# Loading x in four row blocks (12, 8, 8, 4) in a cached grouped-query attention kernel

## The chip, the cores and the metric

The kernel runs on one core of one Trainium2 chip. The metric is the device time of one execution in microseconds (us). The kernel before was run five times; in one more view, a profiled execution shows every engine's instructions and every DMA packet.

## The reference, cut to what matters

Decoding attention over a cache of keys and values, for 8 sequences with 4 new tokens each, 32 query heads, 8 key/value heads, a cache of 2048 positions, head size 128, all in bf16:

```python
B, Sq, D = 8, 4, 512
Hq, Hkv, Sk, Dh = 32, 8, 2048, 128
q = (x @ wq).reshape(B, Sq, Hq, Dh).transpose(0, 2, 1, 3)
k = jnp.repeat(k_cache, rep, axis=1)          # rep = 4
v = jnp.repeat(v_cache, rep, axis=1)
scores = jnp.einsum("bhqd,bhkd->bhqk", q, k) * (Dh ** -0.5)
p = softmax(scores, axis=-1)
o = jnp.einsum("bhqk,bhkd->bhqd", p, v)
out = o.transpose(0, 2, 1, 3).reshape(B, Sq, Hq * Dh) @ wo
```

x has 32 rows of 512 numbers (32 KB); wq and wo have 4 MB each, the two caches 32 MB each.

## The kernel before, in words

**Units.** The work is cut into 32 units, one for each pair of key/value heads and each sequence: for each of four pairs p, all eight sequences b. A unit reads one k tile and one v tile of 1 MB (`load_k`, L111, and `load_v`, L121), each 128 partitions with 8 KB. There are 7 buffers for k tiles and 6 for v tiles.

**Stages of a unit.** TensorE transposes the k tile (L195, two bf16 numbers taken as one fp32), VectorE or ScalarE copies the result to SBUF (L202, L200), TensorE multiplies it by the queries (`scores`, L256), ScalarE takes the exponential (L266), TensorE sums the probabilities (`norms`, L294) and multiplies by v (`values`, L280), VectorE scales (L311). The values of a unit run six half-units behind its scores. The output projection (`project`, L376) is added up in one PSUM tile over the four pairs; its last part waits for the rows of `wo` that are loaded last (`load_wo`, L141).

**The queries.** x (T = 32 rows, one per token) is transposed by four small TensorE operations (L210) into `xT_sb` (copy at L213), then 128 matmuls with wq (L219) give the queries, which ScalarE scales (L226). Four matmuls (L234) and eight copies (L243) lay them out as the block-diagonal `q_bd` that `scores` needs. All of this stands in TensorE's program after the transposes of the first k tile.

**The loads.** All loads are issued by the SP engine in one list. The order is: k of unit 0, wq (4 MB, L144), x (L145), and then what `load_ready` takes from the list `loads`: for the units from 1 on, first one of eight `wo_e` pieces (L131), then the k tile, then, from the fourth on, a v tile. A `wo_e` piece is 5 rows of 12 KB of wo, put on five partitions; it belongs to the rows of wo that the first pair of heads needs. The first `wo_e` piece waits for the memset of `wo_e` on GpSimd (L171). Near the end of the list stand `wo_n` (L134), `wo_m` (L135) and the eight pieces of `wo_sb` (L141). The two halves of the output are stored by ACT (L431) and SP (L432).

**What makes SP wait.** The framework gives the loads eight semaphores in turn, so that each load first waits until the load eight places before it has landed in full. A load into a buffer that is used again also waits for the engine that reads the buffer. The kernel is written with a manual schedule, so each engine's instructions stand in the order in which the code gives them.

The lines that the change touches:

```python
    load_k(0)
    nc.sync.dma_start(wq_sb[:, :, :], wq.rearrange("(p r) n -> p r n", r=R))
    nc.sync.dma_start(x_sb[:, :], x.flatten_outer_dims())
```

Of the kernel before, what the change touches and what calls it, by code (L numbers as in the profile page):

```python
# [14 lines left out]
def kernel(  # L15
# [9 lines left out]
    nc = tc.nc  # L25
# [51 lines left out]
    x_sb = const.tile([T, D], BF16, name="x_sb")  # L77
# [64 lines left out]

    load_k(0)
    nc.sync.dma_start(wq_sb[:, :, :], wq.rearrange("(p r) n -> p r n", r=R))  # L144
    nc.sync.dma_start(x_sb[:, :], x.flatten_outer_dims())  # L145
    loads = []
    for u in range(NU + KA):
        if 1 <= u <= 8:
# [314 lines left out]
```

The softmax here doesn't subtract the row's maximum and nothing guards it: scores larger than these inputs give would overflow.

## Time and profile before

| What | Value |
|---|---|
| Median of five runs | 189.83 us |
| The five runs | 191.86, 189.22, 189.08, 189.83, 192.39 us |
| Profiled execution, its own time | 189.37 us |
| Its span in the trace | 187.6 us |
| TensorE clock granted, mean | 0.979 |
| Bytes read from HBM | 75.53 MB, 403 GB/s over the span |
| Landing of wq / of x, last increment | 15.50 us / 15.69 us |
| First transpose of x on TensorE | 15.74 us |
| First `scores` matmul | 23.27 us |

The span is from the first instruction to the last in the trace; 1.8 us of the execution's own time lie around it. DVE is VectorE, ACT is ScalarE, PE is TensorE, PEld its weight loads, POOL is GpSimd, SP is SyncE; "SPq" is SP's issue of a DMA. A letter L and a number name a line of the kernel. In the row of the 40 slices a digit is the busy share of a slice in tenths. A load's landing is told by increments of its semaphore, one from each DMA engine that takes part in it, and the trace keeps the time of each; it keeps start, length and size of each DMA packet as well, but not the engine's number.

### The profile page before, as it was taken

Reading aid. Unit: us, or ns where it says so; the run is one execution under the profiler, and the core shown is the slowest. Engines: PE = TensorE matmul, PEld = TensorE weight load, DVE = VectorE, ACT = ScalarE, POOL = GpSimd, SP = SyncE. Lnnn points to the kernel's source line nnn. Section 1 sums busy time; section 2 is a strip of 40 time slices with the busy share of each in tenths; the row PEclk is TensorE's granted clock in tenths of the full one; section 3 lists DMA queues with packets and bytes.
Section 4 is the critical chain, followed back from the end, with each engine's and each line's share of the span. In section 5 each row is a group of like instructions: output and inputs, shape, how many; then the busy total and the mean of one; then the engine's idle time right before and its main releaser. Section 6 shows DMA issues by size and latency. Waiting matters only on the chain.

```text
span 187.6 us, 6431 instructions
## 1 busy us (share of the span) xinstructions
PE 154.5 (82%) x2869; PEld 139.1 (74%) x2899; DVE 112.4 (60%) x218; ACT 86.3 (46%) x170; POOL 6.3 (3%) x9
## 2 busy tenths in 40 slices
PE   0535597799999988999999999968888889998672
PEld 0515397699999877889998888857788888886450
DVE  0580544577777666844777666656666667776320
ACT  2003546656556655444565554445554444454000
POOL 8400000000000000000000000000000000000000
PEclk9999979999999999996999999999999999999998
DMA  5999999999999999999999999999999999999970
GB/s 210 461 447 379 424 424 425 427 417 432 425 418 421 426 423 423 430 419 433 421 419 426 428 423 423 421 425 426 421 428 423 426 425 423 423 428 415 406 294 15
DMA packets 10955, 75.97 MB, mean 405 GB/s; under 512 B 1288, under 2 KB 1416, under 8 KB 2568
## 3 DMA queue, kind: packets, MB, share of 16 engines
q1 hardware_dynamic: 10880, 75.55, 96.1%
q8 instruction: 22, 0.36, 0.7%
q14 instruction: 5, 0.04, 0.1%
q10 hardware_dynamic: 48, 0.02, 0.0%
HBM read 75.53 MB, written 0.03 MB: 403 GB/s over the span
## 4 chain that ended last, share of the span: by engine, by line
DMA 97%; SPq 1%; issue 0%; PE 0%; ACT 0%
DMA k_sb<-in_k_cache_dram 69%; DMA v_sb<-in_v_cache_dram 9%; DMA wq_sb<-in_wq_dram 8%; DMA wo_e<-in_wo_dram 7%; DMA wo_sb<-in_wo_dram 4%; SPq L131 0%; PE out_ps L376 0%; SPq L111 0%; ACT out_sb L430 0%; SPq L121 0%
## 5 line engine op out<-in xcount | busy, mean ns | idle before, releaser
L195 PE MATMUL kp<-ident,k_sb 128*128 128x128 f32 x512 | 83.7, 290 | 16.8 <-POOL ident masks.py:199 7.0
L202 DVE COPY kt<-kp 128x1024 bf16<-128x1024 bf16 x96 | 65.2, 684 | 25.3 <-PE kp L195 23.8
L266 ACT ACTIVATE probs<-s_ps 64x256 bf16<-64x256 f32 x128 | 48.4, 378 | 67.1 <-PE s_ps L256 66.3
L195 PEld LDWEIGHTS kp<-ident,k_sb 128*128 128x128 f32 x512 | 56.5, 145 | 19.6 <-DMA k_sb<-in_k_cache_dram 8.2
L256 PE MATMUL s_ps<-q_bd,kt 128*128 128x64 bf16 x1024 | 43.1, 195 | 3.1 <-ACT kt L200 1.9
L256 PEld LDWEIGHTS <-kt 128*128 128x128 bf16 x1024 | 40.6, 100 | 5.5 <-ACT kt L200 2.2
L280 PEld LDWEIGHTS <-v_sb 128*128 128x128 bf16 x1024 | 34.5, 96 | 9.6 <-DMA v_sb<-in_v_cache_dram 2.1
L200 ACT COPY kt<-kp 128x1024 bf16<-128x1024 bf16 x32 | 32.4, 1012 | 12.6 <-PE kp L195 11.8
L280 PE MATMUL o_ps<-probs,v_sb 128*128 128x32 bf16 x1024 | 35.1, 177 | 1.2 <-DMA v_sb<-in_v_cache_dram 1.1
L302 DVE TENSOR_REDUCE l_sb<-l_ps 128x32 f32<-128x512 f32 x32 | 22.1, 692 | 22.0 <-PE l_ps L294 21.7
L294 PE MATMUL l_ps<-probs,ones 128*128 128x512 bf16 x34 | 12.6, 379 | 1.5
L306 DVE RECIPROCAL r_sb<-l_sb 128x32 f32<-128x32 f32 x32 | 11.3, 353 | 1.1
L311 DVE TENSOR_TENSOR oT<-o_ps,r_sb 128x32 bf16<-128x32 f32 x32 | 5.8, 182 | 1.9 <-PE o_ps L280 1.7
L294 PEld LDWEIGHTS <-ones 128*128 128x128 bf16 x64 | 6.1, 98 | 0.5
L430 ACT CAST out_sb<-out_ps 64x256 bf16<-64x256 f32 x1 | 0.4, 366 | 13.1 <-PE out_ps L376 13.1
L171 POOL MEMSET wo_e<- 64x6144 bf16 x1 | 5.2, 5211 | 0.3 <-POOLq L447 0.3
L376 PE MATMUL out_ps<-wo_sb,oP 128*32 128x256 bf16 x48 | 4.1, 274 | 1.4 <-DMA wo_sb<-in_wo_dram 1.4
L243 DVE CAST q_bd<-pse 64x512 bf16<-64x512 f32 x4 | 2.6, 683 | 4.3 <-PE pse L234 4.3
L178 DVE COPY pick<-ident 128x64 bf16<-128x64 bf16 x4 | 0.6, 220 | 6.5 <-POOL ident masks.py:199 6.5
L376 PEld LDWEIGHTS <-oP 128*32 128x32 bf16 x48 | 2.4, 95 | 2.5 <-issue 2.4
L219 PE MATMUL psq<-xT_sb,wq_sb 128*128 128x32 bf16 x128 | 3.5, 186 | 0.3 <-DVE xT_sb L213 0.3
L219 PEld LDWEIGHTS <-wq_sb 128*128 128x128 bf16 x128 | 3.5, 103 | 0.3 <-issue 0.3
(41 smaller groups left out, 31.1 us busy)
## 6 DMA issues: line engine op xcount, KB each, us to landing
k_sb<-in_k_cache_dram SPq DMA_DIRECT2D x32, 1024.0 KB, 19.5
v_sb<-in_v_cache_dram SPq DMA_DIRECT2D x32, 1024.0 KB, 19.4
wq_sb<-in_wq_dram SPq DMA_DIRECT2D x1, 4096.0 KB, 14.3
wo_sb<-in_wo_dram SPq DMA_DIRECT2D x4, 512.0 KB, 14.8
wo_sb<-in_wo_dram SPq DMA_DIRECT2D x4, 256.0 KB, 9.5
wo_m<-in_wo_dram SPq DMA_DIRECT2D x1, 512.0 KB
wo_e<-in_wo_dram SPq DMA_DIRECT2D x8, 60.0 KB
x_sb<-in_x_dram SPq DMA_DIRECT2D x1, 32.0 KB
```

What stands on the lines that cost most here:

```text
L195: nc.tensor.transpose(kp[:, j, :], k4[:, w : w + 128], ident4[:, :])
L200: nc.scalar.copy(out=kt2, in_=kp2)
L202: nc.vector.tensor_copy(out=kt2, in_=kp2)
L219: nc.tensor.matmul(psq[:, h, :], lhsT=wq_sb[:, r, hh * 128 : (hh + 1) * 128], rhs=xT_sb[:, r, :], start=(r == 0), stop=(r == R - 1),)
L256: nc.tensor.matmul(s_ps[:, 2 * j : 2 * j + 2, :], lhsT=k_t[:, j % (HC // 4), :, e], rhs=q_bd[:, p, e, b, :, :], start=(e == 0), stop=(e == 1),
L266: nc.scalar.activation(out=pr[rows, hf * HC : (hf + 1) * HC, cols], in_=s_ps[rows, :, cols], func=EXP)
L280: nc.tensor.matmul(o_ps[u][:, :], lhsT=vs[u][:, cc, :], rhs=pr[:, cc, :], start=(cc == 0), stop=(cc == C - 1),)
L294: nc.tensor.matmul(l_ps[:, :, :], lhsT=ones[:, :], rhs=pr[:, c : c + LC, :], start=(c == 0), stop=(c + LC == C),)
L302: nc.vector.tensor_reduce(out=l_sb[:, :], in_=l_ps[:, :, :].rearrange("d c q -> d q c"), axis=AX, op=ADD)
L306: nc.vector.reciprocal(r_sb[:, :], l_sb[:, :])
L311: nc.vector.tensor_tensor(out=oT[(p + 1) // 2][:, :, (p == 2) * 1, b, :], in0=o_ps[u][:, :].rearrange("d (h s) -> d h s", h=HP), in1=r_sbs ...
L376: nc.tensor.matmul(out_ps[half * T : (half + 1) * T, :], lhsT=o, rhs=w[:, half * DH : (half + 1) * DH], start=(p == 0 and r == 0), stop=(p ...
```

## The change

The load of x is cut into four loads by rows: rows 0 to 11, 12 to 19, 20 to 27 and 28 to 31. They go from the same source rows to the same rows of `x_sb`, in the same place of SP's list, behind wq and ahead of the first `wo_e` piece. Nothing else is changed. In the built programs TensorE, VectorE, ScalarE and GpSimd keep the same instructions in the same order; SP issues three loads more. Lines behind the change move down by two.

```diff
     load_k(0)
     nc.sync.dma_start(wq_sb[:, :, :], wq.rearrange("(p r) n -> p r n", r=R))
-    nc.sync.dma_start(x_sb[:, :], x.flatten_outer_dims())
+
+    for a, n in ((0, 12), (12, 8), (20, 8), (28, 4)):
+        nc.sync.dma_start(x_sb[a : a + n, :], x.flatten_outer_dims()[a : a + n, :])
     loads = []
     for u in range(NU + KA):
         if 1 <= u <= 8:
             loads.append(("e", u - 1))
```

## The prediction

> **What bounds the kernel now.** I read the page from the top (busy shares, the queues, the chain that ended last), then the SP engine's timeline of the first 20 us, where the change sits, and last the trace's records of single DMA packets and semaphore increments. The page first:
>
> ```profile
> span 187.6 us, 6431 instructions
> ...
> PE 154.5 (82%) x2869; PEld 139.1 (74%) x2899; DVE 112.4 (60%) x218; ACT 86.3 (46%) x170; POOL 6.3 (3%) x9
> ...
> DMA  5999999999999999999999999999999999999970
> ...
> q1 hardware_dynamic: 10880, 75.55, 96.1%
> q8 instruction: 22, 0.36, 0.7%
> q14 instruction: 5, 0.04, 0.1%
> ...
> DMA 97%; SPq 1%; issue 0%; PE 0%; ACT 0%
> ```
>
> The DMA row is full from the second slice to the second last, queue q1 alone fills 96.1% of 16 engines' span, and 97% of the chain is DMA. PE is 82% busy and idles for data. So the end is set by bytes through the 16 DMA engines. The windows say the same for the middle (columns: stretch, length, PE, PEld, DVE, ACT, POOL busy, PE clock, DMA share, GB/s):
>
> ```profile
> 40.00:100.00 60.00, 57.30 (x1082) 53.79 (x1095) 42.15 (x85) 33.20 (x67) 0.00 (x0) 0.97 1.01 424
> ```
>
> The chain in order of time ends so (start, length, what):
>
> ```profile
> 176.56 7.53 DMA wo_sb<-in_wo_dram
> 184.09 0.04 issue
> 184.13 0.41 PE out_ps L376 x4
> 184.54 0.02 issue
> 184.56 0.37 ACT out_sb L430
> ```
>
> The last load lands at 184.09; what follows it (four matmuls, one copy, the store) is the same 3.5 us whatever happens earlier.
>
> One level lower: the packet records show every engine back to back. An 8 KB packet takes 309 ns, 12 KB 460 ns, 1 KB 46 ns, the 4 B semaphore packet 9 ns, 16 KB of instructions about 0.95 us. From 14.5 to 18.5 us each chain of packets follows without a gap. The 16 increments of the last load come at 178.8, 178.9, 179.0, 181.3, 181.4, nine between 182.4 and 183.0, 183.88 and 184.09. So the end belongs to one or two engines, and the mean over the 16 is 182.0. Which engines are late can be followed too: each of the eight `wo_e` loads (5 rows of 12 KB) shows five late increments, always behind the same five engines, about 0.45 us each; at 48 us these five land the v load at 47.5 to 47.95, the other eleven at 44.4 to 46.2. The two last engines at the end are, followed load by load, two of these five.
>
> The start, by SP's timeline (start, length of the issue):
>
> ```profile
> 0.73 0.37 SPq L111 DMA_DIRECT2D k_sb<-in_k_cache_dram  x1
> 1.16 0.42 SPq L144 DMA_DIRECT2D wq_sb<-in_wq_dram  x1
> 1.62 0.43 SPq L145 DMA_DIRECT2D x_sb<-in_x_dram  x1
> 5.97 0.84 SPq L131 DMA_DIRECT2D wo_e<-in_wo_dram  x1
> 6.85 0.40 SPq L111 DMA_DIRECT2D k_sb<-in_k_cache_dram  x1
> 7.30 0.72 SPq L131 DMA_DIRECT2D wo_e<-in_wo_dram  x1
> 8.06 0.43 SPq L111 DMA_DIRECT2D k_sb<-in_k_cache_dram  x1
> ...
> 15.52 0.33 SPq L121 DMA_DIRECT2D v_sb<-in_v_cache_dram  x1
> ```
>
> Here SP is idle from 2.05 to 5.97 (the memset of `wo_e` on POOL), and after 9.73 it stands until 15.52:
>
> ```profile
> SPq L121 <- DMA wq_sb<-in_wq_dram: 5.8, 1, 5.8
> ```
>
> In the built program SP's loads take eight semaphores in turn, so load n waits for the full landing of load n-8: the tenth load (v of unit 0) waits for the second (wq, landed at 15.50).
>
> **What the Trainium skill says.** Page "DMA: Bandwidth & Descriptors", section "Why a DMA increments its semaphore by 16 and not by 1": a load issued from SP runs on k engines, the largest k up to 16 that divides the outer sizes, and these are the lowest-numbered k; the sequencer writes the missing 16-k increments at once. The trace agrees on k: `wo_e` with 5 rows shows five late increments and one early, 1.1 to 1.2 us after its issue. That they are the lowest-numbered the trace can't say, only that they are always the same five; I take the page's word. Same page, "Latency and other measured facts": about 600 ns to the first byte from an SP issue; here it is 1.0 us (issue 0.73, first packet 1.73) and 0.85 us for the final store (184.95 to 185.80). Same page, "Rules for kernel authors": under 64 KB one pays mostly overhead. Inside this stream that isn't what one sees: the 32 KB of x cost each engine two 1 KB packets and a semaphore packet, 2 x 46 + 9 = 101 ns, with the next packet directly behind.
>
> **The change, part by part.**
>
> *Bytes on the engines.* Removed: one load of 32 rows on 16 engines, 101 ns of each. Added: loads of 12, 8, 8 and 4 rows, on k = 12, 8, 8 and 4 engines, one row and one semaphore packet (46 + 9 = 55 ns) on each. By the page's rule engines 0-3 take part in all four (220 ns), 4-7 in three (165), 8-11 in one (55), 12-15 in none. The difference is +119, +64, -46 and -101 ns. The five engines that carry `wo_e` are then 0-4, so the two that end last gain +64 to +119 ns. At least one of the two is in 0-3. I take +0.1 us at the end; from both sides 0 and +0.2 (if a packet's gap appears four times instead of once; the increments of x came 0.19 to 0.30 us after those of wq, of which 101 ns was packets).
>
> *Three more issues on SP.* The x issue took 0.43 us, the 5-row `wo_e` issues 0.70 to 0.84; at 0.74 each, four take 3.0 us, from 1.62 to 4.6. `wo_e` waits for POOL until 5.94 anyway. Cost nothing; the cover ends when the four take over 4.3 us.
>
> *Three more places in the eight semaphores.* Numbers of the loads: k0 0, wq 1, x 2-5, wo_e 6, k1 7, wo_e 8 (waits k0, landed 5.7), k2 9. k2 now waits for wq: issued at 15.52 instead of 8.06, behind it a `wo_e`, k3 (9.29 before), v0, a `wo_e`, k4, v1, each held only by a piece of x or by a load already landed. SP's run is then k2 0.43, wo_e 0.70, k3 0.44, v0 0.33, wo_e 0.70, k4 0.44, with 0.04 between: k4 at about 18.4 (16.63 before), v1 at 18.8 (18.31), after which every load waits for the same load as before. What hides it: at 15.5 each engine holds k1, whose packets end at 17.0 to 17.6 on eleven engines and at 17.85 on the five, which have 0.46 us of `wo_e` then. k2's first packet at 15.52 + 1.0 = 16.5 comes 0.5 us before the quickest engine needs it and 1.8 us before the last ones do. k3 follows at 16.7 + 1.0 = 17.7 and is needed from 19.5. Cost nothing; if the cover were gone, each microsecond of dry engine past these margins is one at the end.
>
> *PE's wait.* The transposes of x (L210) began at 15.74 and would begin some 0.1 us later, now after four increments' semaphores. Queued behind: projections, q_bd, first scores at 23.27. DMA waits for PE only through buffers; the waits of SP on PE are 1.0 us in three and 0.8 us in three, none over 0.4, with seven loads queued behind. Nothing.
>
> Sum: +0.1 + 0 + 0 + 0. The profiled execution took 189.37 us (span 187.6 and 1.8 around it), so 189.47; the median of the five runs is 0.46 above it, 189.83, so 189.9.
>
> **Rivals.**
>
> 1. *The queue runs dry behind wq (slower).* Mechanism: at 15.5 one k load is queued instead of three. It decides from an issue-to-packet time over 1.5 us on the quick engines, and 2.8 us on the last five. For: SP issues seven loads in a row there, and nothing shows its latency while engines are full. Against: 0.85 to 1.0 us at both ends of the trace. To pass 1% the five late engines would have to stand 1.9 us: 191.8.
> 2. *The instruction fetches fall otherwise.* 22 packets of 16 KB and 5 of 8 KB share these engines; the two last engines are late by some 0.9 us because of them (jumps near 54, 61, 123 and 165 us), and SP's program grows. One less on both: the next engine is at 183.0, so 1.1 us off, 188.8. One more on a late engine: +0.9, 190.8. PE's program, nearly all of the bytes, is unchanged instruction for instruction. Both stay within 1%.
> 3. *It levels the engines (faster).* If the numbers ran the other way and the last engines were 12-15, they'd lose 101 ns: 189.7. Over 1% would need 1.9 us, nearly all of the 184.09 - 182.01 = 2.1 us that perfect levelling of everything could give, for 4 KB per engine moved at most. Nothing in the profile carries that.
> 4. *The runs themselves.* Two of the five runs before are at 191.86 and 192.39, three at 189.1 to 189.8, with one program. If most runs after fall high, it reads as 191.9.
>
> **How the numbers follow.** Likeliest case 0.74, giving 189.9 (its own range 189.1 to 190.4, the lower three runs and the bounds of the packets). Rival 2 0.10 (188.8 or 190.8), rival 3 with over 1% 0.05, rival 1 0.04, rival 4 0.07. Range to hold 8 in 10: 188.8 to 191.2. About 1% is what a measurement of this kernel can tell from no change. Faster by over 1%: rival 3 and a little of 2, 0.06. Slower: rivals 1 and 4 and a little of 2, 0.12. Within: 0.82.
>
> **What would show it.** In the packets after: 12, 8, 8 and 4 packets of 1 KB, on four engines four of them, 220 ns. In SP's timeline: four x issues done before 5.9, then k2 at about 15.5 and k3 near 16.7, and from k5 (21.2) on the old times. In the increments: k1 and k2 landing within 0.2 us of 17.5 to 18.3 and 20.0 to 21.2, and the last load's slowest increment at 184.1 to 184.3, by one of the five `wo_e` engines. A DMA share under 0.9 between 16 and 20 us, or a last increment over a microsecond away, proves me wrong.

## The result, and the profile after

The kernel after took 189.76 us, the median of 44 runs (188.87 to 191.31). Its ratio to the kernel before is 1.000, with a 95% interval of 0.998 to 1.002. Two later comparisons, each beside its own runs of the kernel before on the same chip, gave 1.0035 (1.0011 to 1.0059) and 1.0046 (1.0034 to 1.0058). In the first comparison 29 of the 79 runs of the kernel before (median 190.87 us) were disturbed and are left out of the ratio, as in every ratio below, but 11 more at 190.87 to 191.67 us count in it; beside the other 39 alone, at 188.92 to 189.90 us with a median of 189.28, the kernel after is 0.25% longer. So the change costs between nothing and half a per cent, within the 1% of "no change".

The time lies in the forecast range, and 189.9 us was close. But the forecast put a term at nothing that is not nothing: the engines did run dry, and in two of the three comparisons a small loss is clear of the noise. By the prediction's own test it was wrong twice: the DMA share fell under 0.9 (0.66 from 17 to 19 us), and in the trace below the last increment came over a microsecond late (185.60 us, forecast 184.1 to 184.3).

The page of the kernel after, its profiled execution at 190.66 us:

```profile
span 188.9 us, 6436 instructions
...
DMA  6998999999999999999999999999999999999981
GB/s 219 448 444 305 384 431 424 422 429 419 429 416 429 416 425 425 423 427 423 429 422 423 427 420 430 416 425 427 423 427 423 423 425 427 420 426 409 371 317 39
...
q1 hardware_dynamic: 10896, 75.55, 96.1%
...
DMA 82%; PE 10%; ACT 3%; DVE 2%; SPq 1%; issue 1%; DVEq 0%
```

The fourth slice holds an 8 in the DMA row and 305 GB/s, with 384 behind it (379 and 424 before). The chain no longer runs through DMA alone: a v load issued at 43.4 us waited last for PE (0.28 us), so the chain follows PE, ACT and DVE from there back to the landing of x. That is not the mark of the gap: the kernel with six loads below has a larger gap and a chain of 95% DMA. Its end, in order of time, is the old one 1.5 us later:

```profile
178.10 7.50 DMA wo_sb<-in_wo_dram
185.60 0.04 issue
185.64 0.41 PE out_ps L378 x4
```

SP's timeline of the start, and the first of its waits that is new:

```profile
1.63 1.62 SPq L147 DMA_DIRECT2D x_sb<-in_x_dram  x4
5.97 0.79 SPq L131 DMA_DIRECT2D wo_e<-in_wo_dram  x1
6.81 0.44 SPq L111 DMA_DIRECT2D k_sb<-in_k_cache_dram  x1
7.30 0.71 SPq L131 DMA_DIRECT2D wo_e<-in_wo_dram  x1
15.37 0.35 SPq L111 DMA_DIRECT2D k_sb<-in_k_cache_dram  x1
15.77 0.70 SPq L131 DMA_DIRECT2D wo_e<-in_wo_dram  x1
16.52 0.44 SPq L111 DMA_DIRECT2D k_sb<-in_k_cache_dram  x1
```

```profile
SPq L111 <- DMA wq_sb<-in_wq_dram: 7.3, 1, 7.3
```

The four x issues, the load that waits for wq (now k2, not v0) and the times 15.4 and 16.5 are as forecast. What follows is not. The windows (columns as in the prediction; the last two are DMA share and GB/s), first of the kernel before, then of the kernel after:

```profile
15.00:17.00 2.00, 0.94 (x28) 0.95 (x29) 0.23 (x1) 0.00 (x0) 0.00 (x0) 1.00 0.99 419
17.00:19.00 2.00, 2.00 (x82) 2.00 (x79) 0.00 (x0) 0.77 (x2) 0.00 (x0) 1.00 1.01 428
19.00:22.00 3.00, 1.87 (x39) 1.03 (x36) 1.39 (x3) 1.85 (x4) 0.00 (x0) 1.00 1.01 425
```

```profile
15.00:17.00 2.00, 0.45 (x11) 0.48 (x12) 0.23 (x1) 0.00 (x0) 0.00 (x0) 1.00 1.05 439
17.00:19.00 2.00, 2.00 (x82) 2.00 (x79) 0.00 (x0) 0.65 (x2) 0.00 (x0) 1.00 0.66 195
19.00:22.00 3.00, 2.41 (x55) 1.45 (x52) 1.13 (x2) 1.30 (x4) 0.00 (x0) 1.00 0.95 381
```

Over these seven microseconds the kernel before moves 838 + 856 + 1275 = 2969 KB, the kernel after 878 + 390 + 1143 = 2411 KB. The missing 558 KB are 1.3 us of a stream of 424 GB/s. They are not made up: from 22 to 40 us the two kernels move 424 and 426 GB/s. The semaphore increments say where (first and last of the 16, us):

```
        before                 after
k1      17.54 ... 18.29        17.47 ... 18.36
k2      19.96 ... 21.17        20.34 ... 22.31
```

k1 is the same; k2 comes up to 1.1 us later. In the packet records, followed as chains, the eleven engines without `wo_e` end k1 at 17.0 to 17.3 us. Nine of them then have no packet for 0.4 to 2.3 us; the other two go on at once, with a first packet that takes 0.8 us in place of 0.31. The five engines with `wo_e` have no idle time there. Counted over all 16 engines from 15.5 to 22.5 us, without following chains, the time without a packet is 13.1 us, and packets that took more than 309 ns took 9.1 us more; in the kernel before both are 0. Together that is 1.4 us for each engine. The engines that stand are those that had slack, which is why not more is lost; but the five lose a little too: the `wo_e` piece behind k2 lands on them at 21.88 to 22.12 us, at 21.28 to 21.63 before. At the end the kernel before had its two latest increments at 183.88 and 184.09, nine between 182.4 and 183.0; the kernel after has five between 185.43 and 185.60. The late group is no longer two of the `wo_e` engines that end 0.9 us behind the rest, it is a level front.

### The profile page after: what moved, and what is told of

Same layout as the page of the kernel before. It is cut to its first block, busy times and chain, and to the rows that moved or that the text cites. A ratio compares the mean times of both kernels' runs of the same rounds, so it can differ in the third digit from the quotient of the medians.

```text
span 188.9 us, 6436 instructions
## 1 busy us (share of the span) xinstructions
PE 157.3 (83%) x2869; PEld 141.0 (75%) x2899; DVE 112.3 (59%) x218; ACT 86.2 (46%) x170; POOL 6.3 (3%) x9
## 4 chain that ended last, share of the span: by engine, by line
DMA 82%; PE 10%; ACT 3%; DVE 2%; SPq 1%; issue 1%; DVEq 0%
DMA k_sb<-in_k_cache_dram 62%; DMA v_sb<-in_v_cache_dram 9%; DMA x_sb<-in_x_dram 7%; DMA wo_sb<-in_wo_dram 4%; PE kp L197 3%; PE s_ps L258 3%; PE psq L221 2%; ACT kt L202 1%; DVE kt L204 1%; DVE q_bd L245 1%; SPq L147 1%; PE o_ps L282 1%; ACT q_bd L245 1%; ACT probs L268 1%; PE pse L236 1%
## 5 line engine op out<-in xcount | busy, mean ns | idle before, releaser
L258 PE MATMUL s_ps<-q_bd,kt 128*128 128x64 bf16 x1024 | 43.6, 197 | 3.0 <-ACT kt L202 1.9
L258 PEld LDWEIGHTS <-kt 128*128 128x128 bf16 x1024 | 41.2, 100 | 5.5 <-ACT kt L202 2.2
L378 PE MATMUL out_ps<-wo_sb,oP 128*32 128x256 bf16 x48 | 4.9, 328 | 0.7 <-DMA wo_sb<-in_wo_dram 0.7
L378 PEld LDWEIGHTS <-oP 128*32 128x32 bf16 x48 | 3.0, 113 | 1.9 <-issue 1.3
## 6 DMA issues: line engine op xcount, KB each, us to landing
v_sb<-in_v_cache_dram SPq DMA_DIRECT2D x32, 1024.0 KB, 19.5
wo_sb<-in_wo_dram SPq DMA_DIRECT2D x4, 512.0 KB, 15.5
```

Source lines behind the costliest of these rows:

```text
L258: nc.tensor.matmul(s_ps[:, 2 * j : 2 * j + 2, :], lhsT=k_t[:, j % (HC // 4), :, e], rhs=q_bd[:, p, e, b, :, :], start=(e == 0), stop=(e == 1),
L378: nc.tensor.matmul(out_ps[half * T : (half + 1) * T, :], lhsT=o, rhs=w[:, half * DH : (half + 1) * DH], start=(p == 0 and r == 0), stop=(p ...
```

## The experiments

Theories on record: **dry queue** (the three more loads take places in the eight semaphores, k2 goes out only when wq has landed, and engines stand; slack hides part of it); **placement** (what counts is which engines carry the rows of x); **small loads or instruction fetches** (the loads cost by themselves, or the gap doesn't bear on the time). All ratios are to runs of the kernel before on the same chip.

| kernel | k2 issued, us | GB/s, 17 to 19 us | median, us | ratio (95%) |
|---|---|---|---|---|
| before | 8.1 | 428 | | 1 |
| before, again | 8.1 | | 189.29 | 0.999 (0.997 to 1.001) |
| after | 15.4 | 195 | 189.76 | 1.000 (0.998 to 1.002) |
| after, again | 15.4 | 268 | 190.30 | 1.0035 (1.0011 to 1.0059) |
| after, third | 15.5 | 248 | 190.18 | 1.0046 (1.0034 to 1.0058) |
| four loads by columns | 15.3 | 285 | 190.47 | 1.0050 (1.0031 to 1.0069) |
| three loads in padding | 15.3 | 317 | 190.71 | 1.0061 (1.0043 to 1.0078) |
| four loads ahead of wq | 8.1 | 424 | 189.51 | 0.999 (0.997 to 1.002) |
| three loads behind wq | 8.1 | | 189.17 | 0.997 (0.995 to 0.999) |
| three loads, again | 8.1 | 424 | 189.25 | 0.9995 (0.9986 to 1.0004) |
| four loads, k ahead of wo_e | 6.8 | | 189.11 | 1.000 (0.998 to 1.001) |
| the same, again | 6.8 | 412 | 189.21 | 0.9986 (0.9966 to 1.0005) |
| six loads behind wq | 16.5 (k1: 15.3) | 360 (15 to 17: 63) | 191.97 | 1.0109 (1.0072 to 1.0146) |

(GB/s is given where there is a trace of an execution near the median.)

**The kernel before and the kernel after, again.** 

> The kernel before, unchanged, for a second trace of it and for its spread. Every theory: ratio 1.0. The dry-queue theory: again no gap between k1 and k2 on any engine, k2 landing 19.9 to 21.3 us, the DMA share over 0.9 from 16.5 to 20 us. If k2 landed past 22 us here too, the dry gap would not come from the change. The last load's slowest increment tells how far the end moves between two executions of one program: the rival that the instruction fetches set it expects steps of about 1 us between profiles.

> The kernel after, unchanged, for a second trace and its spread beside the next kernels. Ratio 0.998 to 1.004. Dry-queue theory: k2 again issued near 15.4 us and landing past 21.3 us on most of the eleven engines without wo_e; if this execution is one of about 189.2 us, its gap between k1 and k2 is smaller than in the first trace (190.66 us), or its late engines are the five with wo_e. Rival that the gap doesn't bear on the time: a gap as large as in the first trace beside 189.2 us.

> The kernel after once more, beside the other three: ratio 1.0 to 1.004 to the kernel before, 189.5 to 190.4. It is the yardstick for the places-only kernel and for the one with k ahead of wo_e.

The repeat of before differs from its own other runs by 0.1%, within its interval. Its trace is of an execution at 192.03 us, far from its median, and is used for SP's issues only. Both repeats of after show the gap again: 5.1 and 11.7 us without a packet, 12.9 and 8.4 us in long packets, by the count above (the third's ratio is a little past the expected 1.004). The first comparison of after had 23 of its 44 runs below 190 us; all three of its traces are of executions at 190.2 to 190.7 us, so what an execution of 189.2 us looked like stays open.

**The same places, other engines.** x cut by columns, each load on 16 engines:

```diff
+    for a in range(0, D, 128):
+        nc.sync.dma_start(x_sb[:, a : a + 128], x.flatten_outer_dims()[:, a : a + 128])
```

> x in four loads as in the change, but cut by columns (32 rows of 256 bytes each), so that every load is spread over all 16 engines. Dry-queue theory: four loads take four places, whatever their rows are, so k2 is issued near 15.4 and lands 20.3 to 22.3 us with most engines idle 1 to 2 us around 17 to 19 us, as in the kernel after; time within 0.3% of the kernel after (189.3 to 190.3). Rival that the rows on the low-numbered engines matter: the end differs from the kernel after by over 0.5 us and the late engines are others.

The gap is there, the time is 0.5% above before. Median and gap are as the dry queue expects (the median 0.17 us past its upper bound), though the rows lie on all engines. Placement isn't what makes the gap.

**The same rows, other places.** The four loads ahead of wq; and, in another kernel, left where the change put them, but with each k tile ahead of its `wo_e` piece, so that k2 is the ninth load and waits for k0:

```diff
-        if 1 <= u <= 8:
-            loads.append(("e", u - 1))
         if 0 < u < NU:
             loads.append(("k", u))
+        if 1 <= u <= 8:
+            loads.append(("e", u - 1))
```

> The same four row loads, issued ahead of wq in place of behind it, so that k2 and k3 wait for pieces of x that landed long before and not for wq. Dry-queue theory: k2 and k3 are issued before 10 us, no engine stands between k1 and k2, the DMA share stays over 0.9 from 15 to 20 us, and what the gap cost is given back: 188.9 to 189.6, at or below the kernel before; if the gap was fully hidden, the same time as after. Rival of row placement: the packets of x are on the same engines as in the kernel after, so the time is the one after.

> The kernel after with one edit: in the list of loads each k tile stands ahead of its wo_e piece. The four row loads stay where they are, but k2 is now the ninth load and waits for k0, not for wq. Dry-queue theory: k1 and k2 are both issued before 9 us, the gap is gone, 189.0 to 189.5, at or below the kernel before and 0.3 to 1 us below the kernel after. Rival that the four small loads themselves cost the time: as the kernel after.

> The kernel after with each k tile ahead of its wo_e piece, once more for an undisturbed trace: k2 issued before 8 us, no gap around 17 to 19 us, 189.0 to 189.4. Rival that the four small loads cost the time: 190.

All three are level with the kernel before, and 0.4 to 0.6% below the kernel after of the later comparisons. The four small loads themselves, with their issues, packets and semaphores, cost nothing that can be measured. The last one's timeline and windows:

```profile
1.62 1.59 SPq L147 DMA_DIRECT2D x_sb<-in_x_dram  x4
3.25 0.36 SPq L111 DMA_DIRECT2D k_sb<-in_k_cache_dram  x1
5.97 0.81 SPq L131 DMA_DIRECT2D wo_e<-in_wo_dram  x1
6.82 0.44 SPq L111 DMA_DIRECT2D k_sb<-in_k_cache_dram  x1
15.39 0.71 SPq L131 DMA_DIRECT2D wo_e<-in_wo_dram  x1
16.14 0.44 SPq L111 DMA_DIRECT2D k_sb<-in_k_cache_dram  x1
```

```profile
15.00:17.00 2.00, 0.41 (x9) 0.44 (x10) 0.23 (x1) 0.00 (x0) 0.00 (x0) 1.00 1.06 448
17.00:19.00 2.00, 2.00 (x80) 2.00 (x79) 0.00 (x0) 0.60 (x2) 0.00 (x0) 1.00 0.98 412
19.00:22.00 3.00, 2.30 (x57) 1.50 (x54) 1.09 (x2) 1.30 (x4) 0.00 (x0) 1.00 1.03 430
```

The same four x loads stand there at 1.62, but two k tiles go out before 7.3 us, and the stream holds: 896 + 824 + 1290 = 3010 KB. k2 lands from 19.92 to 20.75, no engine is without a packet from 15.5 to 22.5 us, and long packets cost 0.4 us in all.

**One place fewer, two places more.** Three loads of 16, 8 and 8 rows; six loads of 12, 8, 4, 4, 2 and 2 rows, both behind wq.

> x in three row loads (16, 8, 8) behind wq: one place less than in the change, so k2 waits for k0 alone and goes out near 8 us; k3 is then the first to wait for a piece of x. Dry-queue theory: at wq's landing k1 and k2 are queued, five microseconds of work, no engine stands, and the time is that of the kernel before, 189.0 to 189.7, below the upper half of the runs after. Rival that each more load costs a little: halfway between before and the column kernel, about 189.8 to 190.

> Three row loads (16, 8, 8) once more, for an undisturbed trace and a second ratio: k2 issued near 8 us, no gap, 189.0 to 189.4, ratio 0.995 to 1.0. If it is again below the kernel before with the interval clear of 1, it is the best version so far; if not, the first 0.997 was chance.

> x in six row loads (12, 8, 4, 4, 2, 2) behind wq: now k1 as well waits for wq, and nothing but x and one wo_e piece is queued at 15.4 us. Dry-queue theory: all sixteen engines stand from about 15 us until k1's packets come, 2.5 to 4 us later, the five that carry wo_e too, and the end moves by that: 192 to 194. If an issue reached the engines in the 0.85 to 1.0 us that the prediction used, the gap would be about 1 us: 190.5. Rival that places in the semaphores don't matter: within 0.3% of after.

Three loads leave k2 to wait for k0: no gap, no loss. The 0.997 of the first run didn't come back, so no version here is shown to beat the kernel before. With six loads k1 waits for wq too, and every engine stands (none has a packet from 15.5 to 16.2 us):

```profile
15.00:17.00 2.00, 0.38 (x8) 0.40 (x9) 0.22 (x1) 0.00 (x0) 0.00 (x0) 0.50 0.39 63
17.00:19.00 2.00, 2.00 (x79) 2.00 (x79) 0.00 (x0) 0.57 (x2) 0.00 (x0) 0.50 0.87 360
19.00:22.00 3.00, 2.07 (x58) 1.51 (x55) 1.27 (x2) 1.51 (x4) 0.00 (x0) 0.78 1.01 411
```

Its stretch of 15 to 22 us moves 126 + 720 + 1233 = 2079 KB, 890 KB or 2.1 us of stream fewer than the kernel before, and its time is 1.1%, 2.1 us, longer (1.4 to 2.8 us by the interval, 2.7 us by the medians of that comparison). Where no engine is covered, the gap counts in full, as far as these intervals tell. (The column with 0.50 is the granted TensorE clock; the chain of this kernel stays on DMA, so it doesn't set the time.) The median is at the lower end of the expected 192 to 194 us; the gap was shorter than the 2.5 to 4 us expected, as k1's packets began 1.0 to 1.8 us after its issue.

**Without the slack.** In two kernels each `wo_e` piece is 5 rows of 16 bytes; this leaves the first 480 rows of wo out of the projection but for 8 numbers of 40 rows.

```diff
-        nc.sync.dma_start(wo_e[a : a + 17 : 4, :, :], rows[b : b + 17 : 4, :, :])
+        nc.sync.dma_start(wo_e[a : a + 17 : 4, 0, :8], rows[b : b + 17 : 4, 0, :8])
```

> The kernel before with every wo_e piece cut from 5 rows of 12 KB to 5 rows of 16 bytes, at its place in the list; so the first 480 rows of wo are left out of the output projection but for 8 numbers of 40 rows, and the five engines lose their 3.7 us of extra packets. Slack theory: the end falls from the five engines' to that of the others, 1.1 us below the kernel before: 188.0 to 188.5, ratio 0.993 to 0.996.

> The same cut of the wo_e pieces (the first 480 rows of wo left out of the projection but for 8 numbers of 40 rows) in the kernel after. Now no engine has wo_e packets to fill the time behind k1, and no engine has been late before. Slack theory: the dry gap of 1.5 to 2.3 us stands on all sixteen engines and shows in full: 1.5 to 2 us above the light kernel before, 189.6 to 190.4. Rival that the gap is made up by a quicker stream later: within 0.5 us of the light kernel before.

The light kernel before took 188.23 us (0.9928, 0.9904 to 0.9952): the five engines' 3.7 us were worth about 1.4 us of the end by the ratio, a little more than the 1.1 us read from the next engine's increment. The light kernel with four loads took 190.34 us (1.0018, 0.9991 to 1.0045). Between the two lie 2.1 us by the medians, 0.9% or 1.7 us by the ratios; between the full kernels of the same comparison lay 0.35%. The end of the two chains, light before and light four:

```profile
175.94 7.44 DMA wo_sb<-in_wo_dram
183.38 0.04 issue
183.42 0.41 PE out_ps L376 x4
```

```profile
177.86 7.48 DMA wo_sb<-in_wo_dram
185.38 0.41 PE out_ps L378 x4
185.81 0.37 ACT out_sb L432
```

With the extra bytes of the five engines gone, a gap of the same size (550 KB from 15 to 22 us) moves the last landing from 183.38 to 185.34. The time came as expected, but not the detail: the expectation had all sixteen engines stand, and in this trace four do, for 1.5 to 1.7 us; k2 lands on four engines at 22.44 to 22.56 and on the other twelve by 20.47, and at the end two engines come at 185.25 and 185.34, the next at 183.88. So 0.9% without the imbalance stands against 0.35% with it: about half of the gap's cost or more was hidden in the kernel after, with intervals of 0.4 and 0.2 to either side.

**The places alone.** The one load of x as before, and behind it three loads of 64 bytes that nothing reads: first into new spare tiles, then into an old padding tile; and the spare tiles alone, untouched.

```diff
     nc.sync.dma_start(x_sb[:, :], x.flatten_outer_dims())
+    for i in range(3):
+        nc.sync.dma_start(pad0[i : i + 1, :32], x.flatten_outer_dims()[i : i + 1, :32])
```

> The kernel before with its one load of x, and behind it three loads of one row of 64 bytes into spare tiles that nothing reads: the three more places in the eight semaphores alone, no row of x on another engine. Dry-queue theory: k2 is issued near 15.4 us, the gap stands, and the time is that of the kernel after or a little above, 189.8 to 190.5. Rival that the rows on the low-numbered engines earn something that hides the gap's cost: clearly above the kernel after of the same call, by over 0.5 us. Rival that places are harmless: as the kernel before.

> The places-only kernel again, with the three loads of 64 bytes put into a padding tile that the kernel before already has and never reads, so that no other tile's address moves. Dry-queue theory: the gap as in the kernel after, packets of 309 ns again, 189.8 to 190.5. If it stays near 192.7, the three one-engine loads themselves cost over 2 us and the theory of places alone is wrong.

> The kernel before with three spare tiles of 64 bytes allotted and never touched: the same instructions, only the addresses of later tiles move. If the 2.5 us that the places-only kernel lay above the kernel after come from addresses, this one is at 191.5 to 192.5 with packets of 8 KB above 309 ns in the mean; if they come from its small loads, it is the kernel before, 189.3.

The first took 192.72 us (1.0185, 1.0170 to 1.0199), which neither theory had. The spare tiles alone took 191.84 us (1.0126, 1.0110 to 1.0141): allotting them moves the wq, k and v tiles and others behind them by 192 bytes, and that alone costs 1.3%. In the padding tile, with no address moved, the three places cost 0.6%, a little above the expected 190.5; and 1.0185 / 1.0126 = 1.0058 says the same of the first pair. So places alone, without one row of x on another engine, make the gap and its cost. Against the kernel after (1.0035 and 1.0046) they lie 0.15 to 0.25% higher with overlapping intervals: if the placement of the rows earns anything, it is that little, and it is not settled. Nor does the size of the gap in one trace rank the times: from 15 to 22 us the kernel with columns lacks 344 KB and the one with the padding 308 KB, the kernel after 558 KB, yet its ratios are the lowest of the three. That a held-back k2 costs time is shown; how much of a gap reaches the end is not.

## Why the prediction was right and wrong, by its steps

- *Bytes on the engines, +0.1 us.* The semaphores count 12, 8, 8 and 4 increments, as worked out. The 0.1 us can't be seen in the time; kernels with the same four loads and no gap are level with before. Nothing contradicts it.
- *Three more issues on SP, nothing.* Right as an issue cost: four issues in 1.62 us (forecast 3.0), done at 3.25, ahead of 5.97.
- *Three more places, "cost nothing".* This is the step that failed: the term was put at nothing, and it costs 0 to 0.5%. The order of waits, the issue at 15.4 and the moment when the quick engines end k1 (17.0 to 17.3; forecast from 17.0) were right. What failed is the term "15.52 + 1.0 = 16.5": the time from k2's issue to its first packets was 1.6 to 4.1 us (15.37 to between 17.0 and 19.5). I took 0.85 to 1.0 us from the first k load and the last store, two moments when nothing else was in the engines, and used it in the middle of the stream, though rival 1 said that "nothing shows its latency while engines are full". Also the first packet of such a late load often takes longer than 309 ns, up to 1.9 us. So k2 landed up to 1.1 us past the forecast, and k5 went out at 22.33 us and not at 21.2.
- *Who pays.* The same step gave the quickest engines a margin of 0.5 us and the five `wo_e` engines one of 1.8 us. The five did not stand, but behind k2 they were 0.4 to 0.5 us late (the last of them lands its `wo_e` piece at 21.63 us before, at 22.12 after, at 22.09 and 21.99 in the repeats); the rows of x explain 0.1 us of that by the prediction's own sum. The others had at least 1.1 us of slack at the end (183.02 against 184.09). What the step didn't do is to set gap and slack against each other: a gap up to 2.3 us against 1.1 us of slack leaves about 1 us; measured are 0 to 0.9. That 189.9 us held is therefore luck in this step: it took the gap for absent, and the slack hid about half of it.
- *Rival 1.* Its mechanism came true at its first threshold (over 1.5 us on the quick engines), and its price of 191.8, with the late five standing too, is what the six-load kernel shows: 191.97. Its chance of 0.04 joined two different things, a gap on eleven engines and a gap on all.
- *PE's wait.* The transposes of x began at 16.2 in place of 15.74, 0.5 us later (forecast 0.1): the four loads' last increments come 0.2 us apart, at 15.54, 15.73, 15.91 and 16.10. No effect on the end is seen, since the kernels with k ahead of `wo_e` have the same four loads behind wq and no loss. The list of SP's waits for PE left out two kinds, 0.5 and 0.2 us in total; nothing hangs on them.

## What to carry to other kernels

Where loads share a fixed number of semaphores, count places, not only bytes: a tiny load behind a big one can hold back the load that was to keep the engines busy, and the harm begins with the one that pushes a big load past its last free place (three loads here: no loss; four: 0 to 0.5%; six: 1.1%). Price a late issue from the middle of a running stream, not from an idle chip. And look at each engine's last increment before you call a gap harmless: slack on one engine can hide a gap there, not on the others.

## What the runs showed of the hardware that was not expected

Issue to first packet was 0.85 to 1.0 us at the two ends of the trace before, 1.0 to 1.8 us for k1 with six loads (15.27 to between 16.3 and 17.0, when all engines were dry), and 1.6 to 4.1 us for k2 in the kernel after, beside engines still at work. Why the last is so long isn't settled.

Addresses matter more than the change: with spare tiles that nothing touches, the built program puts the wq, k and v tiles 192 bytes past a multiple of 512. The median 8 KB packet then takes 312 ns in place of 309, 85% of them are over 311 ns (0.8% before), and the whole stream is slower, here from 40 to 176 us, before and with the spare tiles:

```profile
40.00:176.00 136.00, 124.82 (x2384) 114.00 (x2411) 92.27 (x181) 70.68 (x140) 0.00 (x0) 0.99 1.01 424
```

```profile
40.00:176.00 136.00, 121.45 (x2357) 111.30 (x2382) 91.82 (x178) 69.56 (x138) 0.00 (x0) 1.00 1.01 418
```
